# Dealing VectorE's work on a half out over the feed-forward slots, with clusters found a half ahead

## The chip, the cores and the metric

The kernel runs on one core of one Trainium2 chip. The metric is the device time of one execution in microseconds, the median of three runs. The engines are named as in the profile: PE is TensorE (PEld its weight loads), DVE is VectorE, ACT is ScalarE, POOL is GpSimd, SP issues the DMAs.

## The reference

Clustered attention is followed by a two-layer feed-forward network. Batch 4, 8 heads, 768 positions, head width 64, 16 clusters per head; feed-forward 3072 tokens, width 512, hidden width 2048.

```python
q_assign = argmax(einsum(q_n, c_n)); k_assign = argmax(einsum(k_n, c_n))   # nearest of 16 centroids
mask   = q_assign[:, :, :, None] == k_assign[:, :, None, :]
scores = where(mask, q @ k.T / sqrt(D), -1e9)
attn   = softmax(scores);  attn_out = attn @ v              # (B, H, S, D)
x = attn_out.transpose(0, 2, 1, 3).reshape(B * S, H * D)    # 3072 x 512
h = x @ w_in
g = maximum(h, 0) + alpha * minimum(h, 0)
out = g @ w_out
```

A query attends only to keys of its own cluster.

## The kernel before

**Tiling.** Two heads form a *pair* n; there are 16 pairs, four for each batch b. A pair's 768 queries are taken in two *halves* of 384. Scores are held transposed, keys on partitions: a *chunk* c (0 to 5) is 128 keys by 2 heads by 384 queries. For one half of one pair the work is:

- TensorE computes the six chunks of scores (L461), ScalarE takes their exponential into a tile E (L479, L482).
- VectorE masks E (L494): where the query's cluster differs from the key's, E becomes zero. Two instructions for each chunk, one for each head.
- TensorE weighs v with the masked E (`weigh`, L567).
- VectorE adds the six chunks up (`add_up`, L505 and L510, five adds), turns the sum in 32 by 32 blocks (L515) and reduces it along its rows (L518, `part`, called the row sums below).
- TensorE's small matmul `total` (L527) finishes the denominators from `part`; VectorE's `invert` (L537 to L544) takes reciprocals and turns them; `normalise` (L588) multiplies the weighed sum by them into xT.

In the first batch's pairs (n < 4) the mask is done by extra matmuls (L471) in place of L494.

**Feed-forward.** When the four pairs of one batch have done one half, 384 rows of xT are ready, and a queue `ffn` gets 28 *pieces* for them: 16 of `hidden(f)` (four matmuls L611; ScalarE makes gT and neg, L618 and L619; VectorE joins them by the slope, L603) and 12 of `final` (four matmuls L631; after two of them ScalarE copies the result to y, L637, or VectorE adds it to y, L639). The order is eight hiddens, six finals, eight hiddens, six finals. The slope of hidden f is issued in the piece of the next hidden, ahead of that one's ScalarE work, and in its own piece where f is the last of four. These pieces run during the attention of the next four halves, so that TensorE always has matmuls.

**Order.** The order of instructions on each engine is written out by hand (`manual_schedule`): each engine executes in the order of the code. Steps u count thirds of a half. There are two loops. The first (u up to 23) does the first batch, with the conversion of the double-precision weights spread over it. The second (u from 24, `TOGETHER`) does the other 24 halves, here called *visits*: three steps of five slots, of which a clump of attention work takes the first three. The clump holds the first three chunks' scores, the weighing of the visit before, the masks of those three chunks, the normalise of the visit before, and the adds; then the other three chunks' scores, masks, adds, turn and row sums. Twelve slots are left, numbered 1 to 12 here (two in step 0, five in step 1, five in step 2), and each may get a feed-forward piece. At 28 pieces over 48 slots, the usual places are slots 1, 2, 4, 6, 7, 9 and 11. `total` stands at the head of slot 8, `invert` at the end of slot 9. So visits alternate: seven hiddens, then one hidden with six finals.

**Preparation.** From the second batch on, each pair is prepared while earlier visits run, by pieces at fixed slots counted from its first step: its loads, then `prep_blocks` (VectorE turns q and k, two of L330, slots 10 and 11), `prep_sims` (TensorE, L348, slot 1, and one slot later VectorE's argmax over clusters, L356 to L370), `prep_clusters` (TensorE spreads the winning cluster over partitions, L393; ScalarE copies it, L397; VectorE makes the keys, L404 and L408), and `prep_queries` for each half (VectorE, L425, slots 10 and 11 of the visit before it, called the query turns). In the kernel before, sims stand in slot 1 and clusters in slot 5 of the visit just before the pair's first. `total`, `prep_sims` and `prep_clusters` share one PSUM bank (`ps_m`, one buffer); hiddens and finals rotate through two (`ps_f`), which also take the third and fourth chunk's scores.

Of the kernel before, what the change touches and what calls it, by code (L numbers as in the profile page):

```python
# [9 lines left out]
FP32 = mybir.dt.float32  # L10
# [4 lines left out]
ALU = mybir.AluOpType  # L15
AX = mybir.AxisListType
PS = bass.MemoryType.PSUM
P = 128
# [3 lines left out]
def kernel(  # L22
# [11 lines left out]
    nc = tc.nc  # L34
# [4 lines left out]
    NJ = S // P  # L39
    NCH = DM // P  # L40
    NF = DF // P
    HJ = NJ // 2
    HS = HJ * P
    SCALE = float(D) ** -0.5
    GROUP = 2
# [19 lines left out]
    accp = fast.enter_context(tc.tile_pool(name="accp", bufs=2))  # L65
    rdp = fast.enter_context(tc.tile_pool(name="rdp", bufs=1))
# [36 lines left out]
    Q = 32  # L103
# [41 lines left out]
    for g in range(P // Q):  # L145
        r = slice(g * Q, (g + 1) * Q)
        nc.gpsimd.tensor_copy(
            out=fold[r, :].rearrange("p (a i) -> p a i", i=Q),
# [178 lines left out]
    def prep_blocks(n, w):  # L327
        if w == 0:
            qkTs[n] = qkp.tile([P, NB * P], FP32, name="qkT")
        nc.vector.transpose(out=qkTs[n][:, w * S:(w + 1) * S],  # L330
                            in_=raw_qk[n, w].rearrange("p j h d -> p (j h d)"))
        square(n, w)
# [11 lines left out]
    def prep_sims(n):  # L344
        hp = pairs[n][1]
        ps = misc()
        for g in range(NG):
            nc.tensor.matmul(out=ps[g * W:(g + 1) * W, 0:HS],  # L348
                             lhsT=cT[:, hp * W:(hp + 1) * W],
                             rhs=qkTs[n][:, g * HS:(g + 1) * HS],  # L350
                             start=True, stop=True)
        later(1, lambda: prep_argmax(n, ps))
# [34 lines left out]
    def prep_clusters(n):  # L387


        first = firsts.pop(n)  # L390
        ps = misc()
        for g in range(NG):
            nc.tensor.matmul(out=ps[:, g * 2 * NX:(g + 1) * 2 * NX], lhsT=spread[:, g, :],  # L393
                             rhs=first, start=True, stop=True)
        every = fsp.tile([P, NG, GT, NG, 2], BF16, name="every")
        everys[n] = every
        later(1, lambda: nc.scalar.copy(every.rearrange("p g i r h -> p (g i r h)"),  # L397
                                        ps[:, 0:NG * 2 * NX]))
        later(2, lambda: prep_keys(n))
# [42 lines left out]
    def more_room():  # L442
        for raw in raw_tiles:
            e_tiles.insert(0, raw.rearrange("p n w -> p (n w)").bitcast(FP32)[
                :, 0:2 * HS].rearrange("p (h q) -> p h q", h=2))
# [39 lines left out]
    def last(m):  # L485

        return waiting[len(waiting) - m:]

    def mask(m):
        for n, half, c, E in last(m):  # L490
            if n < NCH:
                continue
            for h in range(2):
                nc.vector.scalar_tensor_tensor(  # L494
                    out=E[:, h, :], in0=aqs[n, half][:, h, :],
                    scalar=keys[n][:, NJ + c, h:h + 1],
                    in1=E[:, h, :], op0=ALU.is_equal, op1=ALU.mult)

    def add_up(m):

        n, half, c, _ = last(m)[0]
        E = [e for _, _, _, e in last(m)]
        if c == 0:
            acc = accp.tile([P, 2, HS], FP32, name="acc")
            nc.vector.tensor_tensor(out=acc, in0=E[0], in1=E[1], op=ALU.add)  # L505
            accs[n, half] = acc
            E = E[2:]
        acc = accs[n, half]
        for e in E:
            nc.vector.tensor_tensor(out=acc, in0=acc, in1=e, op=ALU.add)  # L510
        if c + m == NJ:


            accT = accp.tile([P, 2 * NX, Q], FP32, name="acc")
            nc.vector.transpose(out=accT.rearrange("p x i -> p (x i)"),  # L515
                                in_=acc.rearrange("p h q -> p (h q)"))
            part = rdp.tile([P, 2 * NX], FP32, name="part")
            nc.vector.tensor_reduce(out=part, in_=accT, axis=AX.X, op=ALU.add)  # L518
            parts[n, half] = part

    parts, totals = {}, {}

    def total(n, half):

        if (n, half) in parts:
            ps = misc()
            nc.tensor.matmul(out=ps[:, 0:2 * NX], lhsT=fold, rhs=parts.pop((n, half)),  # L527
                             start=True, stop=True)
            totals[n, half] = ps
# [134 lines left out]
    AHEAD = 4  # L664
# [3 lines left out]
    for (n, half), u in start_of.items():  # L668
        def at(step, slot, piece):
            prep_at.setdefault((step, slot), []).append(piece)  # L670
        if half == 0:
            load_at.setdefault(max(u - AHEAD - 3, -AHEAD), []).append(n)
            if n < NCH:
                for g in range(len(groups)):
                    at(u - 4, FIRST + g, lambda n=n, g=g: prep_features(n, g))
            else:
                for w in range(2):
                    at(u - 4, FIRST + w, lambda n=n, w=w: prep_blocks(n, w))
            at(u - 3, FIRST, lambda n=n: prep_sims(n))
            if n >= NCH:  # L680
                at(u - 2, FIRST, lambda n=n: prep_clusters(n))
        for h in range(2):
            at(u - 1, FIRST + h, lambda n=n, half=half, h=h: prep_queries(n, half, h))

# [15 lines left out]
    for u in range(-AHEAD, TOGETHER):  # L700
        for n in load_at.get(u, []):
            if n > 1:
                load(n)
        n, half, s = steps[max(u, 0)]
        prior = steps[max(u - 1, 0)]
        ended = u > 0 and prior[2] == SB - 1
        tick()
        if u >= 0:
            score(n, half, range(s * GROUP, (s + 1) * GROUP))
        tick()  # L710
        if ended:
            invert(*prior[:2])
        if u > 0:
            weigh(GROUP, denominators=u <= UB)
        if u >= 0:
            mask(GROUP)
        if ended:
            normalise(*prior[:2])
        if u >= UB:
            add_up(GROUP)  # L720
        if u == UB:
            early.clear()
            feed_block(u)
            whole = len(ffn) - KEEP
        take = (max(len(ffn) - KEEP - whole * (UB - 1 - u % UB) // UB, 0) if ffn else 0)
        converting = 0 if u < 0 else 1 + (u % 4 == 3) if u < UB else 1 + u % 2
        for i in range(SLOTS - FIRST):
            tick()
            feed(take * (i + 1) // 3 - take * i // 3)
            if (u, i) == (1 - AHEAD, 0):  # L730
                cT, alpha_neg = prepare_constants()
            prepare(u, FIRST + i)
            if i < converting:
                convert_next()
        if s == SB - 1 and u >= UB:
            total(n, half)
    assert not sources and not under_way and not unfinished[0]
    more_room()
    for u in range(TOGETHER, NS + 1):
        for n in load_at.get(u, []):  # L740
            load(n)
        if u < NS:
            n, half, s = steps[u]
        if s == 0 or u == NS:
            prior = steps[u - 1][:2]
            assert not unfinished[0]
            tick()
            if u < NS:
                score(n, half, range(0, NJ // 2), alone=NJ // 2 - 1)
            tick()  # L750
            invert(*prior)
            weigh(GROUP if u == TOGETHER else NJ)
            if u < NS:
                mask(NJ // 2)
            normalise(*prior)
            if u % UB == 0:
                feed_block(u)
                whole = len(ffn) - (NS - u <= UB)
            if u == NS:
                break  # L760
            add_up(NJ // 2)
            tick()
            score(n, half, range(NJ // 2, NJ), alone=NJ // 2)
            mask(NJ // 2)
            add_up(NJ // 2)
            slots = range(3, SLOTS)
        else:
            slots = range(SLOTS)
        for i in slots:
            tick()  # L770
            if s == 0:
                prepare(u, FIRST + i - 3)
            if (s, i) == (SB - 1, 0):
                total(n, half)
            at_slot = (u % UB) // SB * FREE + (s * SLOTS + i - 3)
            left = UB // SB * FREE - 1 - at_slot
            pieces = len(ffn) - (NS - u <= UB) - whole * left // (UB // SB * FREE)
            feed(max(pieces, 0))
            if (s, i) == (SB - 1, SLOTS - 1) and unfinished[0]:
                feed(1)  # L780
            if s > 0:
                prepare(u, i)
            if (s, i) == (SB - 1, 1):
                invert(n, half)
    assert not prep_at
    while due:
        tick()
    good = const.tile([P, 2], FP32, name="good")
# [169 lines left out]
```

## Time and profile before

| | |
|---|---|
| time, median of 3 runs | 1061.76 us (1061.55 to 1062.21) |
| span of the profiled execution | 1057.3 us |
| granted TensorE clock | 0.995 |
| first loop | 0 to about 209.7 us |
| second loop, 24 visits | 209.7 to about 967 us |
| last feed-forward block alone | from about 967 us |
| VectorE busy within 470 to 860 us | 267.0 of 390 us |
| TensorE busy within 470 to 860 us | 373.3 of 390 us |

How to read it: a profile line of the timeline gives start, length, engine, line, operation, tiles written and read, shapes and count; in square brackets stands the idle time of the engine before it and what ended that. In the list of waits a line tells who waited for whom: total, number of times, longest. A matmul in 32-bit floats appears as two records; their ends are modelled, and the next record normally starts before the last one's modelled end.

Durations on VectorE that the change touches, mean of one: mask 611 ns (L494), add 957 ns (L510), turn 978 ns (L515), row sums 952 ns (L518), slope 666 ns (L603), block turn 939 ns (L330), query turn 568 ns (L425), y sum 684 ns (L639).

### The profile page before, as it was taken

The page shows a single profiled execution, that of the slowest core. Times are in us where ns is not written, and L with a number is a line of the kernel's source. Part 1 is how long each engine was busy: PE and PEld are TensorE (multiplying, and loading weights), DVE is VectorE, ACT ScalarE, POOL GpSimd, SP SyncE. Part 2 cuts the span into 40 slices and gives each one's busy share as a digit, 9 for nine tenths or more (in the row PEclk, how much of TensorE's full clock was granted, in tenths as well). Part 3 has the DMA queues.
Part 4 walks back from the last instruction along what each step waited for, and adds up shares of the span by engine and source line. Part 5 has one row for each costly group of instructions (what it writes and reads, how often), then busy time and mean ns, then how long its engine had stood idle before and what let it go on. Part 6 is the DMA issues. An engine that isn't in the chain of part 4 may idle for free.

```text
span 1057.3 us, 10220 instructions
## 1 busy us (share of the span) xinstructions
PE 1008.8 (95%) x3827; PEld 488.5 (46%) x3827; DVE 679.3 (64%) x1155; ACT 346.4 (33%) x676; POOL 55.9 (5%) x71
## 2 busy tenths in 40 slices
PE   8999999789999999999999999999999999999997
PEld 4444444344444545444444454544444454544553
DVE  4896878778475756757777573767857576661111
ACT  5655434334331323323133241413333032330220
POOL 1332312200000000000000000000000000000000
PEclk9999999899999999999999999999999999999999
DMA  9542654020000230050000230014000000000000
GB/s 219 175 126 80 140 111 90 20 59 11 1 1 20 40 45 16 1 105 15 1 1 0 61 40 5 15 35 85 1 0 1 23 8 0 1 1 30 1 1 33
DMA packets 120936, 42.72 MB, mean 40 GB/s; under 512 B 113696, under 2 KB 113712, under 8 KB 120880
## 3 DMA queue, kind: packets, MB, share of 16 engines
q1 hardware_dynamic: 120704, 41.95, 18.5%
q8 instruction: 32, 0.52, 0.2%
q14 instruction: 24, 0.20, 0.1%
q10 hardware_dynamic: 176, 0.04, 0.0%
HBM read 35.69 MB, written 6.29 MB: 40 GB/s over the span
## 4 chain that ended last, share of the span: by engine, by line
PE 71%; DVE 24%; issue 1%; ACT 1%; DMA 1%; SPq 0%; POOL 0%; DVEq 0%; POOLq 0%; ACTq 0%
PE fps L631 24%; PE fps L611 24%; PE vps L567 11%; PE sps L461 7%; DVE acc L510 7%; DVE raw L494 3%; DVE E L494 2%; PE fps L461 2%; DVE acc L515 2%; DVE part L518 2%; DVE acc L505 1%; DVE gT L603 1%; PE sps L471 1%; PE fps L562 1%; DVE xT L588 1%
## 5 line engine op out<-in xcount | busy, mean ns | idle before, releaser
L631 PE MATMUL fps<-w_out_sb,gT 128*128 128x512 f32 x768 | 342.4, 598 | 14.8 <-DVE gT L603 8.2
L611 PE MATMUL fps<-xT,w_in_sb 128*128 128x384 f32 x1024 | 343.6, 491 | 2.8 <-DVE y L639 2.8
L611 PEld LDWEIGHTS fps<-xT,w_in_sb 128*128 128x128 f32 x1024 | 190.4, 190 | 144.1 <-ACT raw L482 4.4
L631 PEld LDWEIGHTS fps<-w_out_sb,gT 128*128 128x128 f32 x768 | 143.1, 190 | 192.6 <-issue 154.5
L618 ACT ACTIVATE gT<-fps 128x384 f32<-128x384 f32 x128 | 62.9, 491 | 270.3 <-PE fps L611 270.3
L603 DVE SCALAR_TENSOR_TENSOR gT<-neg,alpha_neg,gT 128x384 f32<-128x384 f32 x128 | 83.1, 666 | 97.9 <-ACT neg L619 97.5
L494 DVE SCALAR_TENSOR_TENSOR raw<-aq,key,raw 128x384 f32<-128x384 bf16 x160 | 87.3, 611 | 44.3 <-ACT raw L482 44.3
L461 PE MATMUL sps<-qkT 64*128 64x384 f32 x576 | 110.5, 502 | 0.0
L482 ACT ACTIVATE E<-sps 128x768 f32<-128x768 f32 x88 | 67.2, 813 | 82.2 <-PE sps L471 44.9
L494 DVE SCALAR_TENSOR_TENSOR E<-aq,key,E 128x384 f32<-128x384 bf16 x128 | 70.3, 611 | 20.5 <-ACT E L482 20.5
L567 PE MATMUL vps<-E,vt 128*64 128x384 f32 x448 | 81.4, 491 | 0.0
L639 DVE TENSOR_TENSOR y<-y,fps 128x512 f32<-128x512 f32 x30 | 20.5, 684 | 91.9 <-PE fps L631 91.9
L461 PEld LDWEIGHTS sps<-qkT 64*128 64x128 f32 x576 | 52.0, 187 | 51.3 <-issue 21.1
L510 DVE TENSOR_TENSOR acc<-acc,E 128x768 f32<-128x768 f32 x64 | 61.2, 957 | 19.1 <-ACT E L482 16.9
L619 ACT ACTIVATE neg<-fps 128x384 f32<-128x384 f32 x128 | 62.1, 485 | 16.6 <-DVE gT L603 16.6
L482 ACT ACTIVATE raw<-sps 128x768 f32<-128x768 f32 x56 | 42.9, 814 | 70.1 <-PE sps L461 70.1
L637 ACT COPY y<-fps 128x512 f32<-128x512 f32 x24 | 14.1, 586 | 141.7 <-PE fps L631 141.7
L567 PE MATMUL vps<-raw,vt 128*64 128x384 f32 x320 | 56.5, 491 | 0.0
L567 PEld LDWEIGHTS vps<-E,vt 128*64 128x64 f32 x448 | 30.4, 137 | 41.3 <-issue 41.1
L510 DVE TENSOR_TENSOR acc<-acc,raw 128x768 f32<-128x768 f32 x48 | 45.8, 955 | 1.1
L461 PE MATMUL fps<-qkT 64*128 64x384 f32 x192 | 41.4, 508 | 0.0
L588 DVE TENSOR_TENSOR xT<-vps,rd 128x384 f32<-128x384 f32 x32 | 17.8, 557 | 33.9 <-PE vps L567 33.4
(100 smaller groups left out, 663.7 us busy)
## 6 DMA issues: line engine op xcount, KB each, us to landing
raw<-in_moe_w_in_dram SPq DMA_DIRECT2D x16, 512.0 KB, 4.2
raw<-in_moe_w_out_dram SPq DMA_DIRECT2D x16, 512.0 KB, 3.6
vt<-in_v_dram SPq DMA_DIRECT2D x16, 384.0 KB, 4.8
out_dram<-y SPq DMA_DIRECT2D x24, 256.0 KB, 2.0
qk<-in_q_dram SPq DMA_DIRECT2D x48, 96.0 KB, 3.5
qk<-in_k_dram SPq DMA_DIRECT2D x48, 96.0 KB, 3.7
qk<-in_q_dram SPq DMA_DIRECT2D x8, 192.0 KB, 4.9
qk<-in_k_dram SPq DMA_DIRECT2D x8, 192.0 KB, 4.5
```

The costliest lines, as they stand in the source:

```text
L461: nc.tensor.matmul(out=bank(ps, h), lhsT=qkT[r:r + D, S + c * P:S + (c + 1) * P], rhs=qkT[r:r + D, half * HS:(half + 1) * HS], start=True, ...
L482: nc.scalar.activation(out=E, in_=ps[:, :, 0:HS], func=AF.Exp, scale=SCALE)
L494: nc.vector.scalar_tensor_tensor(out=E[:, h, :], in0=aqs[n, half][:, h, :], scalar=keys[n][:, NJ + c, h:h + 1], in1=E[:, h, :], op0=ALU.is ...
L510: nc.vector.tensor_tensor(out=acc, in0=acc, in1=e, op=ALU.add)
L515: nc.vector.transpose(out=accT.rearrange("p x i -> p (x i)"), in_=acc.rearrange("p h q -> p (h q)"))
L567: nc.tensor.matmul(out=po[r:r + D, 0:HS], lhsT=vts[n][:, h, c, :], rhs=e[:, h, :], start=(c == 0), stop=(c == NJ - 1))
L588: nc.vector.tensor_tensor(out=xTs[b, half][:, hp, :], in0=pos.pop((n, half))[:, 0:HS], in1=rds.pop((n, half)), op=ALU.mult)
L603: nc.vector.scalar_tensor_tensor(out=gs[f], in0=neg, scalar=alpha_neg[:, f:f + 1], in1=gs[f], op0=ALU.mult, op1=ALU.add)
L611: nc.tensor.matmul(out=ps[:, 0:HS], lhsT=w_in_sb[:, c, f * P:(f + 1) * P], rhs=xT[:, c, :], start=(c == 0), stop=(c == NCH - 1))
L618: nc.scalar.activation(out=gs[f], in_=ps[:, 0:HS], func=AF.Relu)
L619: nc.scalar.activation(out=neg, in_=ps[:, 0:HS], func=AF.Relu, scale=-1.0)
L631: nc.tensor.matmul(out=ps[:, 0:DM], lhsT=gs[f][:, i * P:(i + 1) * P], rhs=w_out_sb[:, f, :], start=on and f == f0, stop=off and f == f0 + ...
```

## The change

Its first part takes work of VectorE out of the clump of the second loop. The clump keeps the masks of the first three chunks and the normalise. The masks of the other three chunks, all five adds, the turn and the row sums go into a list `todo`, along with `total` and `invert`: twelve items, of which each of the visit's twelve slots does one at its end. So slots 1 to 3 mask chunks 3 to 5, slots 4 to 8 add, slot 9 turns, slot 10 takes the row sums, slot 11 has `total` and slot 12 `invert`. It is meant to let the feed-forward's slopes and y sums, and the argmax, through on VectorE without a long clump of attention work in front of them.

Its second part finds a pair's clusters earlier. Loads move from 7 to 9 steps ahead of the pair's first step, blocks from 4 to 7, sims from 3 to 6, clusters from 2 to 4. Sims are still in slot 1, now two visits ahead, and clusters in slot 10 of that same visit. Queries stay one step ahead. For the pairs next in line this moves some preparation into the first loop.

In the first loop only the form of the helpers changes (an add for each chunk; turn and row sums as functions of their own at the same place).

```diff
-            load_at.setdefault(max(u - AHEAD - 3, -AHEAD), []).append(n)
+            load_at.setdefault(max(u - (7 if n < NCH else 9), -AHEAD), []).append(n)
...
-                    at(u - 4, FIRST + w, lambda n=n, w=w: prep_blocks(n, w))
-            at(u - 3, FIRST, lambda n=n: prep_sims(n))
+                    at(u - 7, FIRST + w, lambda n=n, w=w: prep_blocks(n, w))
+            at(u - (3 if n < NCH else 6), FIRST, lambda n=n: prep_sims(n))
             if n >= NCH:
-                at(u - 2, FIRST, lambda n=n: prep_clusters(n))
+                at(u - 4, FIRST, lambda n=n: prep_clusters(n))
...
             if u < NS:
-                mask(NJ // 2)
+                for chunk in last(NJ // 2):
+                    mask(chunk)
             normalise(*prior)
...
-            add_up(NJ // 2)
             tick()
             score(n, half, range(NJ // 2, NJ), alone=NJ // 2)
-            mask(NJ // 2)
-            add_up(NJ // 2)
+            E = last(NJ)
+            for c in range(NJ // 2, NJ):
+                todo.append(lambda c=c, E=E: mask(E[c]))
+            for c in range(1, NJ):
+                todo.append(lambda c=c, E=E: add_up(E[c], E[c - 1]))
+            todo.append(lambda n=n, half=half: turn(n, half))
+            todo.append(lambda n=n, half=half: rows_sums(n, half))
+            todo.append(lambda n=n, half=half: total(n, half))
+            todo.append(lambda n=n, half=half: invert(n, half))
...
-            if (s, i) == (SB - 1, 0):
-                total(n, half)
...
-            if (s, i) == (SB - 1, 1):
-                invert(n, half)
-    assert not prep_at
+            todo.popleft()()
+    assert not prep_at and not todo
```

More of the change, by code (lines that the diff above doesn't have):

```diff
@@ L487, in last, with mask @@
         return waiting[len(waiting) - m:]
[L489 to L502, printed above, removed]
+    def mask(chunk):
+        n, half, c, E = chunk
+        if n < NCH:
+            return
+        for h in range(2):
+            nc.vector.scalar_tensor_tensor(
+                out=E[:, h, :], in0=aqs[n, half][:, h, :],
+                scalar=keys[n][:, NJ + c, h:h + 1],
+                in1=E[:, h, :], op0=ALU.is_equal, op1=ALU.mult)
@@ L503, in add_up @@
+    def add_up(chunk, former):
+        n, half, c, E = chunk
         if c == 0:
[L504 to L507, printed above, removed]
+            return
+        if c == 1:
+            accs[n, half] = accp.tile([P, 2, HS], FP32, name="acc")
         acc = accs[n, half]
-        for e in E:
-            nc.vector.tensor_tensor(out=acc, in0=acc, in1=e, op=ALU.add)
@@ L511, in add_up @@
[L511 to L519, printed above, removed]
+        nc.vector.tensor_tensor(out=acc, in0=former[3] if c == 1 else acc, in1=E,
+                                op=ALU.add)
@@ L521, with turn, rows_sums @@
+    def turn(n, half):
+        accT = accp.tile([P, 2 * NX, Q], FP32, name="acc")
+        nc.vector.transpose(out=accT.rearrange("p x i -> p (x i)"),
+                            in_=accs.pop((n, half)).rearrange("p h q -> p (h q)"))
+        accTs[n, half] = accT
+    def rows_sums(n, half):
+        part = rdp.tile([P, 2 * NX], FP32, name="part")
+        nc.vector.tensor_reduce(out=part, in_=accTs.pop((n, half)), axis=AX.X, op=ALU.add)
+        parts[n, half] = part
+    accTs = {}
     parts, totals = {}, {}
@@ L715 @@
         if u >= 0:
-            mask(GROUP)
+            for chunk in last(GROUP):
+                mask(chunk)
         if ended:
@@ L719 @@
         if u >= UB:
-            add_up(GROUP)
+            add_up(last(1)[0], last(2)[0]) if s == 0 else [
+                add_up(chunk, None) for chunk in last(GROUP)]
+            if s == SB - 1:
+                turn(n, half)
+                rows_sums(n, half)
         if u == UB:
@@ L738 @@
     more_room()
+    todo = deque()
     for u in range(TOGETHER, NS + 1):
@@ L753 @@
             if u < NS:
-                mask(NJ // 2)
+                for chunk in last(NJ // 2):
+                    mask(chunk)
             normalise(*prior)
```

## The prediction

> **What bounds the kernel now.** I read the page first, then the list of waits kept to TensorE, then the timeline round the places where those waits fall.[...]
>
> ```profile
> span 1057.3 us, 10220 instructions
> PE 1008.8 (95%) x3827; PEld 488.5 (46%) x3827; DVE 679.3 (64%) x1155; ACT 346.4 (33%) x676; POOL 55.9 (5%) x71
> ...
> q1 hardware_dynamic: 120704, 41.95, 18.5%
> ```
>
> TensorE sets the end: no other engine is over 64%, and the queue for loads is at 18.5%. The change takes no matmul away, so it can only win time in which TensorE stands still. The list of waits, TensorE alone, gives that time by cause (us in total, times, longest):
>
> ```profile
> PE mps L393 <- DVE first L370: 18.5, 10, 2.3
> PE fps L631 <- DVE gT L603: 8.2, 12, 1.0
> PE fps L631 <- POOL w_out_sb L253: 6.7, 2, 3.5
> PE fps L611 <- DVE y L639: 2.8, 2, 2.4
> ```
>
> Three of the four end on VectorE, an engine that is only 64% busy: VectorE is late in places, not short of time. Two stretches of the timeline (start, length, engine, line, operation) show why. The first is a visit with a new pair's clusters in it:
>
> ```profile
> 477.46 2.93 DVE L510 TENSOR_TENSOR acc<-acc,E 128x768 f32<-128x768 f32 x3
> ...
> 480.42 0.98 DVE L515 STREAM_TRANSPOSE acc<-acc 128x768 f32<-128x768 f32 x1
> ...
> 481.44 0.95 DVE L518 TENSOR_REDUCE part<-acc 128x24 f32<-128x768 f32 x1
> 482.31 0.57 DVE L356 STREAM_TRANSPOSE simT<-mps 128x384 f32<-128x384 f32 x1
> ...
> 484.49 0.55 DVE L370 TENSOR_REDUCE first<-top 128x24 bf16<-128x384 bf16 x1
> ...
> 485.10 0.26 PE L393 MATMUL mps<-first,spread 128*128 128x24 bf16 x4 [2.34 <-DVE first L370]
> ```
>
> The argmax (L356 to L370) stands behind the whole clump of sums, turn and row sums, and the cluster matmul of slot 5 stands waiting for it. The second is a visit of finals:
>
> ```profile
> 635.62 0.98 DVE L515 STREAM_TRANSPOSE acc<-acc 128x768 f32<-128x768 f32 x1
> ...
> 636.63 0.95 DVE L518 TENSOR_REDUCE part<-acc 128x24 f32<-128x768 f32 x1
> 637.50 1.14 DVE L603 SCALAR_TENSOR_TENSOR gT<-neg,alpha_neg,gT 128x384 f32<-128x384 f32 x2
> ...
> 638.16 8.85 PE L631 MATMUL fps<-w_out_sb,gT 128*128 128x512 f32 x20 [1.01 <-DVE gT L603]
> ```
>
> Here the two slopes, whose inputs ACT had finished at about 632.9, come behind turn and row sums, and the second final waits.
>
> [...] The operations keep their shapes, so I use the trace's durations.
>
> **What is removed.** The idle times count from a matmul's modelled end, though the next one normally starts before it: in a running stream records are 0.32 us apart and 0.49 us long. So each wait costs about 0.16 us more than listed: 18.5 + 10 x 0.16 = 20.1 for L393; 8.2 + 12 x 0.16 = 10.1 for the slopes, of which 0.4 lies at 98 us in the first loop and stays; 2.8 + 2 x 0.16 = 3.1 for the y sums.
> - L393: blocks still come one step before sims, but clusters now follow sims by nine slots (1 to 10), not four (1 to 5). VectorE's argmax (2.6 us) has the length of six feed-forward pieces, over 15 us, and no clump of sums in front of it. I take all 20.1 as gone.
> - Slopes: with mask, sums and turn out of the clump, VectorE is free after the normalise (600.92 in the visit that starts its pieces at 602.38). A slope now stands ahead of its own slot's dealt item, and slope 7 ahead of all of them, so it ends 4.4 us (3.75 until neg is ready, 0.65) after its hidden starts; the final that needs it starts at 2.6 + 3.4 = 6.0. All 9.7 gone.
> - y sums at 223 to 229 us, behind the first masked clump: gone for the same reason, 3.1.
> Sum removed: 33 us.
>
> **What is added.** The dealt items are the same instructions, so VectorE's 679 us stays. Turn and row sums, though, move from just after the clump to slots 9 and 10, and the total (TensorE, L527) from slot 8 to slot 11, straight behind them. TensorE now waits in order for row sums; behind it stand the last pieces and the next scores. I walk the instruction order of the changed kernel, with t = 0 at the first hidden. Hiddens follow each other every 2.58 us (ACT's L618 starts at 605.27, 607.85, 610.43), and neg of hidden k is ready at 3.75 + 2.58k (606.13 - 602.38 for the first). Back to back and with their hand-overs an add takes 0.99, turn 1.01, row sums 0.97, slope 0.60, query turn 0.58, block turn 0.95 (spacing of starts around 606 to 612; L330 for the last).
> - Five visits of seven hiddens: the fourth hidden's slope ends at 3.75 + 7.74 + 0.65 = 12.15. Then three adds, a slope, turn, a query turn, row sums: 2.97 + 0.60 + 1.01 + 0.58 + 0.97 = 6.13, so 18.3. TensorE reaches the total at 7 x 2.58 + 0.1 = 18.15. Wait 0.2 each, 1.0.
> - Four such visits that also hold sims, clusters and a block turn: TensorE 18.15 + 0.8 + 0.2 = 19.15; VectorE 18.3 + 0.8 + 0.95 = 20.05. Wait 0.9 each, 3.6.
> - Two visits where the total comes after six hiddens (the third and the last but one of the loop): VectorE 12.15 + two adds 1.98 + turn 1.01 + slope 0.60 + query 0.58 + row sums 0.97 = 17.3; TensorE 15.6. Wait 1.7 each, 3.4.
> - The loop's first visit, where the cluster matmul and the total follow the fifth hidden: 12.15 + 1.01 + 0.58 + 0.95 + 0.97 = 15.65 against 13.1. Wait 2.55.
> - Twelve visits with finals, 3.44 us each (eight records 0.43 apart): TensorE reaches the total at 2.6 + 6 x 3.44 = 23.2, in two of them after five finals at 19.8. VectorE is held by the second y sum until 17.2 (fourth final's end 16.4 and 0.7); two adds, turn, query and row sums bring it to 21.7, in the two without the adds to 19.8. No wait.
> Together 10.5 us. The later invert (reciprocal, minimum, two turns, 1.6 us) ends about 1 us into the next scores' masks; the normalise then still ends by the time the weighing does (626.9 in the trace), so it is hidden by the weighing. Earlier blocks, sims and clusters put 5.2 us more on VectorE in the first loop; its gap of 2.6 us at 155.2 and the next ones take it up, save 0.5 us in the step with the weights' wait (POOL, 6.7), where the keys now stand ahead of the last conversion: +0.5. Loads move two steps earlier and have a whole visit to land against 3.5 us; nothing.
>
> The unknown cost is the wait at the total. Bounds: zero in all visits, or one more dealt item (1 us) of lag in each of the twelve hidden visits.
>
> **The rivals.**
> 1. No wait at the total, since VectorE runs a little ahead of my walk: 1061.8 - 33 + 0.5 = 1029.3. For it: the five plain visits miss by only 0.2. Against: the fourth hidden's slope pins the rest.
> 2. VectorE lags more, because each dealt item stands behind a slope that waits for ACT: one more us in twelve hidden visits, 1039.8 + 12 = 1051.8.
> 3. A wait takes the place of the ones removed: the first visit's 2.55 us at the total in all 24 visits, 61 us, against 33 + 0.5 gained and paid: 1061.8 - 33 + 0.5 + 61 = 1090, slower. For it: the total now has one slot, not eight slots, of room behind row sums. Against: the walk leaves 1.5 us of room in ten of the twelve visits with finals.
>
> **How the numbers follow.** Forecast 1061.8 - 33 + 10.5 + 0.5 = 1039.8, chance 0.60. Rival 1: 0.14. Rival 2: 0.19. Rival 3, with milder forms that still end slower: 0.05; in between and unchanged, 0.02. The range takes rivals 1 and 2 at their ends, 1029 to 1052. Faster 0.93, same 0.02, slower 0.05.
>
> **What would show it.** Right: the list of waits has no cluster matmul on first and no final on gT past the first loop, and a new entry of the total's matmul on part, about 10 us, with its longest near 2.4 early in the second loop. TensorE's busy time stays within a few us of 1009. Wrong: that entry over 30 us, or new waits of hiddens on xT, of scores, or of weighing on masks; a gain under 10 us without such an entry would mean that the removed waits were no cause.

## The result, and the profile after

The changed kernel takes 1035.96 us (median of four runs, 1032.79 to 1039.08) against 1061.99 us: ratio 0.9754, 95% interval 0.9724 to 0.9785. That is 26 us gained. The two profiled executions are 22.7 us apart (spans 1057.3 and 1034.6 us): the profiled execution of the kernel before took 1059.04 us, 3 us under the median, at a granted clock of 0.995.

From the page of the changed kernel, the span and the busy times:

```profile
span 1034.6 us, 10221 instructions
PE 1007.1 (97%) x3827; PEld 494.2 (48%) x3827; DVE 674.6 (65%) x1155; ACT 345.5 (33%) x676; POOL 55.7 (5%) x71
```

Every engine has as many instructions as before and, within 1.2%, the same busy time; the span alone is shorter. So what went is time in which TensorE stood still. The list of TensorE's waits in the changed kernel (who waited for whom: us in total, times, longest):

```profile
PE fps L634 <- POOL w_out_sb L253: 7.0, 2, 3.6
PE mps L530 <- DVE part L520: 5.2, 7, 2.1
PE fps L614 <- POOL w_in_sb L253: 3.1, 1, 3.1
...
PE fps L634 <- DVE gT L606: 0.2, 1, 0.2
```

(L634, L614 and L530 are the finals, the hiddens and `total`, which were L631, L611 and L527.) The cluster matmul is gone from the list, and so are the hiddens behind a y sum; of the finals behind a slope one of 0.2 us at 98 us is left. Two entries are new: `total` waits for the row sums in seven visits, and one hidden waits for w_in in the first loop, that is for GpSimd's last step (L253) of converting a block of that weight.

A visit of the changed kernel with a cluster matmul in it, in order of time:

```profile
488.17 0.61 DVE L606 SCALAR_TENSOR_TENSOR gT<-neg,alpha_neg,gT 128x384 f32<-128x384 f32 x1
488.70 0.97 DVE L514 STREAM_TRANSPOSE acc<-acc 128x768 f32<-128x768 f32 x1
488.83 0.25 PE L393 MATMUL mps<-first,spread 128*128 128x24 bf16 x4
488.94 2.83 PE L614 MATMUL fps<-xT,w_in_sb 128*128 128x384 f32 x8
...
490.05 0.94 DVE L330 STREAM_TRANSPOSE qkT<-qk 128x768 f32<-128x768 f32 x1
...
490.91 0.91 DVE L520 TENSOR_REDUCE part<-acc 128x24 f32<-128x768 f32 x1
...
491.97 0.37 PE L530 MATMUL mps<-part,fold 128*128 128x24 f32 x2 [0.20 <-DVE part L520]
```

The cluster matmul has no bracket: it waits for nothing. The turn now stands near the visit's end, the block turn between it and the row sums, and `total` comes 0.20 us too early. In the second loop's first visit the same order costs ten times that:

```profile
240.91 0.62 DVE L606 SCALAR_TENSOR_TENSOR gT<-neg,alpha_neg,gT 128x384 f32<-128x384 f32 x1 [1.37 <-ACT neg L622]
241.45 0.97 DVE L514 STREAM_TRANSPOSE acc<-acc 128x768 f32<-128x768 f32 x1
...
242.39 0.25 PE L393 MATMUL mps<-first,spread 128*128 128x24 bf16 x4
...
243.66 0.91 DVE L520 TENSOR_REDUCE part<-acc 128x24 f32<-128x768 f32 x1
...
244.72 0.37 PE L530 MATMUL mps<-part,fold 128*128 128x24 f32 x2 [2.08 <-DVE part L520]
```

Here `total` follows the cluster matmul directly, while VectorE has waited until 240.91 for the fourth hidden's neg and has turn, a query turn, a block turn and row sums still to do.

### The profile page after: what moved, and what is told of

It is laid out like the page before. It is cut to its first block, busy times and chain, and to the rows that moved or that the text cites. A ratio compares the mean times of both kernels' runs of the same rounds, so it can differ in the third digit from the quotient of the medians.

```text
span 1034.6 us, 10221 instructions
## 1 busy us (share of the span) xinstructions
PE 1007.1 (97%) x3827; PEld 494.2 (48%) x3827; DVE 674.6 (65%) x1155; ACT 345.5 (33%) x676; POOL 55.7 (5%) x71
## 4 chain that ended last, share of the span: by engine, by line
PE 86%; DVE 8%; ACT 2%; issue 1%; DMA 1%; POOL 1%; SPq 0%; DVEq 0%; POOLq 0%; ACTq 0%
PE fps L634 31%; PE fps L614 28%; PE vps L570 11%; PE sps L461 9%; PE fps L461 4%; DVE acc L508 2%; PE fps L565 1%; PE sps L471 1%; PE mps L348 1%; DVE gT L606 1%; DVE acc L514 1%; DVE qkT L330 1%; DVE part L520 1%; DMA raw<-in_moe_w_in_dram 1%; PE mps L530 1%
## 5 line engine op out<-in xcount | busy, mean ns | idle before, releaser
L614 PE MATMUL fps<-xT,w_in_sb 128*128 128x384 f32 x1024 | 342.7, 492 | 3.1 <-POOL w_in_sb L253 3.1
L634 PE MATMUL fps<-w_out_sb,gT 128*128 128x512 f32 x768 | 337.1, 595 | 7.2 <-POOL w_out_sb L253 7.0
L614 PEld LDWEIGHTS fps<-xT,w_in_sb 128*128 128x128 f32 x1024 | 192.0, 191 | 147.6 <-issue 7.1
L634 PEld LDWEIGHTS fps<-w_out_sb,gT 128*128 128x128 f32 x768 | 144.8, 190 | 184.8 <-issue 166.1
L606 DVE SCALAR_TENSOR_TENSOR gT<-neg,alpha_neg,gT 128x384 f32<-128x384 f32 x128 | 86.2, 676 | 156.2 <-ACT neg L622 155.5
L570 PE MATMUL vps<-E,vt 128*64 128x384 f32 x448 | 81.5, 491 | 0.0
L570 PE MATMUL vps<-raw,vt 128*64 128x384 f32 x320 | 56.5, 491 | 0.0
L570 PEld LDWEIGHTS vps<-E,vt 128*64 128x64 f32 x448 | 30.5, 137 | 41.8 <-issue 41.0
L479 ACT ACTIVATE raw<-fps 128x384 f32<-128x384 f32 x48 | 21.0, 493 | 48.5 <-PE fps L461 48.5
```

Of the source, the lines that this page charges most:

```text
L479: nc.scalar.activation(out=E[:, h, :], in_=ps[h][:, 0:HS], func=AF.Exp, scale=SCALE)
L570: nc.tensor.matmul(out=po[r:r + D, 0:HS], lhsT=vts[n][:, h, c, :], rhs=e[:, h, :], start=(c == 0), stop=(c == NJ - 1))
L606: nc.vector.scalar_tensor_tensor(out=gs[f], in0=neg, scalar=alpha_neg[:, f:f + 1], in1=gs[f], op0=ALU.mult, op1=ALU.add)
L614: nc.tensor.matmul(out=ps[:, 0:HS], lhsT=w_in_sb[:, c, f * P:(f + 1) * P], rhs=xT[:, c, :], start=(c == 0), stop=(c == NCH - 1))
L634: nc.tensor.matmul(out=ps[:, 0:DM], lhsT=gs[f][:, i * P:(i + 1) * P], rhs=w_out_sb[:, f, :], start=on and f == f0, stop=off and f == f0 + ...
```

## The experiments

The theory: TensorE's waits came from the order of VectorE's queue, a clump that stood in front of short operations which TensorE needs. The main rival: the cluster waits, two thirds of the listed 29.5 us, went because clusters are found earlier. The first four runs split the change in two and take its two new costs away one at a time.

**The dealing alone.** The four distances of the preparation are put back:

```diff
-            load_at.setdefault(max(u - (7 if n < NCH else 9), -AHEAD), []).append(n)
+            load_at.setdefault(max(u - AHEAD - 3, -AHEAD), []).append(n)
...
-                    at(u - 7, FIRST + w, lambda n=n, w=w: prep_blocks(n, w))
-            at(u - (3 if n < NCH else 6), FIRST, lambda n=n: prep_sims(n))
+                    at(u - 4, FIRST + w, lambda n=n, w=w: prep_blocks(n, w))
+            at(u - 3, FIRST, lambda n=n: prep_sims(n))
...
-                at(u - 4, FIRST, lambda n=n: prep_clusters(n))
+                at(u - 2, FIRST, lambda n=n: prep_clusters(n))
```

> The dealing alone; loads, blocks, sims and clusters stay where the kernel before has them (clusters four slots after sims). Theory (the order on VectorE is the cause): with no clump of sums in front of it the argmax (2.6 us after slot 1's mask) is done long before slot 5, three pieces or over 7 us later, so L393 waits under 1 us in all; the waits of finals on gT and of hiddens on y go too; total waits on part 6 to 8 us; the w_in wait of 3.1 us in the first loop is gone, since the v loads are issued two steps later again. About 1034 us, like the changed kernel or 2 us better. Rival (finding the clusters earlier is what removes the cluster wait): L393 keeps some 18 us of waits, and the time is about 1054.

Measured: 1034.05 us (five runs, 1031.61 to 1035.13) against 1062.15, ratio 0.9732 (0.9710 to 0.9754). Its list of TensorE's waits begins:

```profile
PE mps L530 <- DVE part L520: 6.6, 7, 2.2
PE fps L634 <- POOL w_out_sb L253: 6.1, 2, 3.5
```

No cluster matmul waits, though clusters are as late as before, and the wait on w_in is gone. The theory holds and the rival falls: the dealing brings 28 us by itself, and no gain from adding the second part to it can be seen.

**The earlier preparation alone.** The kernel before with the second part of the change:

```diff
-            load_at.setdefault(max(u - AHEAD - 3, -AHEAD), []).append(n)
+            load_at.setdefault(max(u - (7 if n < NCH else 9), -AHEAD), []).append(n)
...
-                    at(u - 4, FIRST + w, lambda n=n, w=w: prep_blocks(n, w))
-            at(u - 3, FIRST, lambda n=n: prep_sims(n))
+                    at(u - 7, FIRST + w, lambda n=n, w=w: prep_blocks(n, w))
+            at(u - (3 if n < NCH else 6), FIRST, lambda n=n: prep_sims(n))
...
-                at(u - 2, FIRST, lambda n=n: prep_clusters(n))
+                at(u - 4, FIRST, lambda n=n: prep_clusters(n))
```

> The earlier loads, blocks, sims and clusters alone; masks, sums, turn and row sums stay in the clump, total in slot 8. Both theories: L393's 18.5 us of listed waits go. Theory: the finals' waits on gT (8.2 listed) and of hiddens on y (2.8) stay, and the w_in wait of about 3 us in the first loop appears as in the changed kernel: 1062 - 20 + 4 = about 1046 us. Rival (the waits are all of one kind and the earlier argmax frees VectorE for the slopes as well): gT waits under 3 us, about 1036.

Measured: 1050.04 us (1048.46 to 1051.37), ratio 0.9884 (0.9862 to 0.9906): 12 us gained, 4 fewer than the theory gave, and 14 short of what its rival gave. Its list of TensorE's waits:

```profile
PE fps L631 <- DVE gT L603: 9.0, 13, 1.0
PE fps L631 <- POOL w_out_sb L253: 7.0, 2, 3.5
PE fps L611 <- POOL w_in_sb L253: 3.4, 1, 3.4
PE fps L611 <- ACT neg L619: 3.2, 4, 0.8
PE fps L611 <- DVE y L639: 1.8, 2, 1.4
```

The cluster waits are gone and the slopes' stay, as expected. The fourth line was not expected, and the timeline shows where it comes from:

```profile
424.91 0.55 DVE L370 TENSOR_REDUCE first<-top 128x24 bf16<-128x384 bf16 x1
425.38 2.55 DVE L603 SCALAR_TENSOR_TENSOR gT<-neg,alpha_neg,gT 128x384 f32<-128x384 f32 x4
426.02 0.49 ACT L619 ACTIVATE neg<-fps 128x384 f32<-128x384 f32 x1 [2.32 <-DVE gT L603]
...
426.57 2.85 PE L611 MATMUL fps<-xT,w_in_sb 128*128 128x384 f32 x8 [0.81 <-ACT neg L619]
```

The slopes are held up behind the clump and the argmax; so ScalarE's neg, which has two buffers, waits 2.32 us for a slope, and a hidden waits for the PSUM bank that this neg has to empty. In the kernel before neg waited 2.32 us too in such a visit (until 485.60 us), but TensorE was then standing at the cluster matmul anyway (until 485.10). Taking one wait away laid the next one open. Its 3.2 us, with 0.16 us of overlap for each of the four, are about the 4 us that the theory's gain was too high by.

**The v load back at 7 steps.** The changed kernel, with the v load as a function of its own:

```diff
+        if n < NCH:
+            load_v(n)
+    def load_v(n):
...
+            if n >= NCH:
+                load_v_at.setdefault(max(u - 7, -AHEAD), []).append(n)
...
```

> The changed kernel with only the v load put back to 7 steps ahead, a line of its own; the q and k loads stay 9 steps ahead. Theory (the v load waits in SyncE's queue for the weighing that frees its buffer, and the weights' loads stand behind it): SyncE's stop of some 18 us before 176 us goes, the wait of a hidden on w_in (3.1 us) is gone, the wait on w_out stays near 7: 1036 - 3.3 = about 1032.5 us. Rival (the w_in wait comes from VectorE's extra block turns and argmax in the first loop): the wait stays within 1 us of 3.1 and the time within 1 us of the changed kernel.

In the changed kernel SyncE's queue near the wait on w_in reads, with its entry in SyncE's list of waits on top (the v load waited for a weighing 12 times):

```profile
SPq L125 <- PE vps L570: 202.8, 12, 27.1
...
155.74 2.47 SPq L119 DMA_DIRECT2D qk<-in_k_dram  x4
176.18 0.39 SPq L125 DMA_DIRECT2D vt<-in_v_dram  x1
176.67 2.08 SPq L230 DMA_DIRECT2D raw<-in_moe_w_out_dram  x4
```

and VectorE's and TensorE's:

```profile
182.23 0.43 DVE L235 TENSOR_SCALAR power<-raw 128x512 uint32<-128x512 uint32 x1 [3.86 <-DMA raw<-in_moe_w_out_dram]
...
180.39 2.10 PE L614 MATMUL fps<-xT,w_in_sb 128*128 128x384 f32 x6
185.59 0.59 PE L614 MATMUL fps<-xT,w_in_sb 128*128 128x384 f32 x1 [3.10 <-POOL w_in_sb L253]
```

SyncE issued nothing between 158.2 us (the pair's last k load) and 176.18, where the weighing (L570) of an older pair let its v buffer go; four loads of weights then came at once. VectorE stood 3.86 us for the first of them (until 182.23), and behind that in its queue was its part of the w_in conversion (L250, at 183.51), which GpSimd's part follows at 184.27 and the hidden at 185.59. With the v load later, SyncE's queue reads:

```profile
153.21 2.42 SPq L119 DMA_DIRECT2D qk<-in_k_dram  x4
155.72 16.25 SPq L235 DMA_DIRECT2D raw<-in_moe_w_out_dram  x3
176.08 0.38 SPq L130 DMA_DIRECT2D vt<-in_v_dram  x1
```

Three of those loads now go out before the v load. The wait on w_in is gone, the waits on w_out total 6.1 us and those of `total` still 5.2. Measured: 1030.48 us (1030.15 to 1034.61), ratio 0.9714 (0.9691 to 0.9738). The rival falls, since VectorE's extra work in the first loop is still there and the wait is not. The waits show this; the time is 5.5 us under the changed kernel's, but the two intervals overlap.

**Two items in the slots without a piece.** The changed kernel, with the row sums two slots earlier:

```diff
-            todo.popleft()()
+            slot = s * SLOTS + i - 2
+            for _ in range({3: 2, 5: 2, 9: 0, 10: 0}.get(slot, 1)):
+                todo.popleft()()
```

> The changed kernel with two dealt items in slots 3 and 5 and none in 9 and 10, so that the row sums come in slot 8; total and invert stay in 11 and 12. Theory (total waits only because the row sums are issued one slot ahead of it): the waits of total on part, 5.2 us listed over 7 visits, fall under 0.6, no new wait of finals on gT over 1 us: 1036 - 6 = about 1030 us. Rival (VectorE has no time left in those visits, wherever the items stand): total still waits 3 us or more, or the waits move to gT, and the time is within 2 us of the changed kernel.

Measured: 1029.09 us (1028.06 to 1030.45), ratio 0.9694 (0.9673 to 0.9714). The entry of `total` waiting on part is gone from TensorE's list, and nothing new waits on gT; the first visit alone keeps a wait, of another kind:

```profile
PE fps L634 <- POOL w_out_sb L253: 6.9, 2, 3.5
PE fps L614 <- POOL w_in_sb L253: 2.4, 1, 2.4
...
PE mps L530 <- ACT every L397: 1.0, 1, 1.0
```

There `total` follows the cluster matmul directly and has to wait until ScalarE has emptied their common bank. VectorE had the time; the row sums stood too late in its queue. The rival, by which 3 us or more of these waits stay, falls.

**Both mends, with either preparation.** The same two items on the dealing alone, and on the changed kernel with the later v load.

> The dealing alone (preparation where the kernel before has it) with two items in slots 3 and 5 and none in 9 and 10. Theory (both remaining costs of the changed kernel are separate: the row sums one slot ahead of total, and the v load in SyncE's queue): total's waits on part (6.6 us listed in the dealing alone) under 0.8, no wait on w_in, w_out near 6.5: 1034 - 7.7 = about 1026.5 us, faster than every kernel so far. Rival (with clusters four slots after sims, the denser slots 3 and 5 put the argmax late again): L393 waits 3 us or more, and the time is 1030 or above.

> The changed kernel with both mends: two items in slots 3 and 5, and the v load 7 steps ahead. Theory: the two gains add, 1036 - 5.5 - 7 = about 1024 to 1026 us; left are the waits on w_out near 6.5 and about 1 us at the first total of the second loop. Rival (they overlap): about 1029 us, as with the two items alone.

Measured: 1024.13 us (1024.06 to 1024.37), ratio 0.9646 (0.9627 to 0.9665), on the dealing alone; 1024.99 us (1024.49 to 1025.16), ratio 0.9653 (0.9634 to 0.9673), on the changed kernel. The two gains add. Of the first, the list of TensorE's waits begins:

```profile
PE fps L634 <- POOL w_out_sb L253: 6.3, 2, 3.5
PE fps L311 <- ACT qkT L315: 1.4, 3, 0.9
```

The 3 us of cluster waits that its rival expected are not in the list, and neither is a wait of `total` on part or of a hidden on y; of the finals behind a slope one of 0.2 us is left. Its median is the lowest of the study: the change's second part taken back, and the row sums earlier.

**Turn and row sums alone.** The kernel before, with only these two out of the clump:

```diff
...
+            if (s, i) == (1, 1):
+                turn(n, half)
+            if (s, i) == (1, 3):
+                rows_sums(n, half)
             if (s, i) == (SB - 1, 1):
                 invert(n, half)
```

> The kernel before with only turn (0.98 us) and row sums (0.95 us) taken out of the clump, into slots 4 and 6; masks, adds, total, invert and the whole preparation stay. Theory (each wait is the excess of the clump over the room behind it, so 1.93 us less in the clump takes 1.93 us from every wait): L393 2.34 falls to about 0.4 where it was longest and to nothing elsewhere, gT waits of 1.0 vanish, the y wait of 2.4 falls to 0.5; about 3 us of the 29.5 listed are left: about 1032 us. Rival (the masks and adds are what makes VectorE late, and turn and row sums only move): half of the waits stay or a wait of total on part takes their place, 1045 us or more.

Measured: 1035.46 us (1033.72 to 1037.96), ratio 0.9756 (0.9733 to 0.9779), as much as the whole change and 3.5 us short of what the theory gave. Its list of TensorE's waits:

```profile
PE mps L534 <- DVE part L525: 2.5, 1, 2.5
...
PE mps L393 <- DVE first L370: 1.7, 5, 0.3
...
PE fps L618 <- DVE y L646: 0.9, 2, 0.5
```

The longest cluster wait fell from 2.3 to 0.3 and the longest y wait from 2.4 to 0.5, each by about the 1.93 us that left the clump, and past the first loop no final waits on gT. So the clump was too long by about the length of these two, and that accounts for most of the old waits. It does not make masks and adds in the clump free: this kernel is 11 us slower than the dealing with the row sums earlier. Its three lines above, which that kernel lacks, are 5.1 us of it; the slow matmuls after the longest wait (last section) belong to it too, and the rest was not located. The first line was not expected. In one late visit `total` follows the fourth hidden, and row sums in slot 6 stand behind that hidden's slope, which waits for ScalarE; it is the same fault as in the changed kernel: row sums that stand too late for `total`.

## Why the prediction was right, and where it was off

1039.8 us was forecast and 1035.96 measured: 22 us of gain against 26.

- *TensorE's standing time bounds the kernel, VectorE is late and not short of time*: right. VectorE's busy time went from 679.3 to 674.6 us, and the waits went. The two items moved inside the visit, at no less work for VectorE, show it again.
- *Removed, 33 us*: right in sum; the three entries left the list, but for the slope at 98 us that was forecast to stay. The prediction gave two reasons for the cluster waits, more slots and no clump in front. Each suffices alone: the dealing without more slots takes these waits away, and so does the earlier preparation with the clump in place. The change had both, so the two gains could not add.
- *Wait of `total` on part, 10.5 us*: the right wait in the right visits, and none in the visits with finals, as forecast; its size was too large. With the 0.16 us of overlap for each, the list gives 5.2 + 7 x 0.16 = 6.3. The first visit cost 2.08 + 0.16 = 2.24 (forecast 2.55), the two where it follows six hiddens 1.3 each (1.7), those with sims and block turn 0.20 + 0.16 = 0.36 (0.9), and the five plain visits nothing (0.2). The mis-sized term is the spacing on VectorE. The walk gave nearly every instruction its full length and a hand-over (turn 1.01, slope 0.60, query turn 0.58, block turn 0.95). In the changed kernel starts lie closer where an instruction does not need the one before it: 0.89 after the turn and 0.46 after the query turn (488.70, 489.59, 490.05), 0.86 after the block turn (490.91), 0.50 after a slope (308.06 to 308.56). The turn's 1.01 came from the kernel before, where the row sums, which need it, follow it directly (635.62 to 636.63). In the visit where `total` waits until 310.02, the row sums end 4.7 us after the fourth hidden's slope, and the walk had 5.14. (A slip of 0.1 without effect: for the visits with finals, 16.4 and 0.7 make 17.1, not 17.2.)
- *Loads: "nothing"*: wrong, by 3.1 + 0.16 us. The prediction asked whether the loads would land in time and not what stands behind them in SyncE's queue. The v load waits for TensorE (issued at 176.18 us, 18 us after the k load before it), and the loads of weights wait behind the v load (issued from 176.67 us on).
- *+0.5 us at the last conversion*: the wait on w_out went from 6.7 to 7.0.
- *Later `invert`, hidden by the weighing*: right; neither weighing nor hiddens wait for it in the list.

The wrong sizes partly cancel: 4.2 us less at `total`, 3.3 more at w_in. That the total came so close is to that extent luck. With the measured sizes the sum is 33 - 6.3 - 3.3 - 0.3, about 23 us, and the two profiled executions are 22.7 apart. The rest of the difference to the 26 us between the medians is about what the runs themselves vary by (6.3 us over four runs of the changed kernel, 6.1 over eleven of the one before), and that goes with the granted clock (last section).

## What to carry to other kernels

Where an engine takes its work in the order of the code, as VectorE did here (in the earlier preparation alone four slopes left from 425.38 us on, behind turn, row sums and argmax, and a neg waited 2.32 us for them), look at what stands between an operation that the bounding engine needs and the head of the queue, not at the share of busy time: 1.93 us out of a clump were worth as much here as dealing most of it out at first was (27 and 26 us). The dealing alone was worth 38 once the row sums stood three slots ahead of `total`. When work moves later, its consumer has to move by as much or the producer has to stand well before it; a row sum one slot ahead of its matmul became the largest wait that the change added (5.2 us). And the v load that waited for its buffer until 176.18 us held up the four loads of weights behind it in SyncE's queue: ask of each prefetch moved earlier what it may block.

## What the runs showed of the hardware that was not expected

After the 2.08 us wait in the second loop's first visit, the eight matmul records of the next hidden took 4.52 us where 2.83 is usual: six of them, from 245.70 us on, started 0.64 us apart where 0.32 is usual. The table by stretches of the changed kernel shows it in the granted clock (after the stretch come its length, then busy time and count for PE, PEld, DVE, ACT and POOL, PEclk, DMA share, GB/s):

```profile
244.93 4.52 PE L614 MATMUL fps<-xT,w_in_sb 128*128 128x384 f32 x8
...
221.00:243.00 22.00, 21.64 (x74) 11.15 (x70) 15.17 (x25) 5.74 (x14) 0.00 (x0) 1.00 0.19 42
243.00:250.00 7.00, 5.28 (x14) 2.89 (x16) 5.23 (x11) 1.10 (x5) 0.00 (x0) 0.76 0.00 0
```

So that wait cost some 1.7 us more than its own length. Over 236 to 252 us the mean clock was 0.89 in the changed kernel and in the dealing alone, whose list has a longest wait of `total` of 2.2 us, and 1.00 in the kernel before and with the two items. In the kernel with only turn and row sums out of the clump, the first two matmul records of the hidden after its 2.5 us wait, from 839.85 us on, took 1.63 us; those of the changed kernel's hidden at 488.94 us took 0.89. It isn't a rule in these runs: after the cluster wait of 2.34 us at 300.2 us in the kernel before, the clock stayed at 1.00 (296 to 306). Nor is it the length alone: the wait on w_in of 3.1 us left the changed kernel at 1.00 (182 to 190), and the 2.08 us were followed by 0.76. And at the waits on w_out where the second loop begins the clock stood at 0.50 for 5 us (205 to 210 us in the kernel before, 210 to 215 in the changed one); over 205 to 221 us its mean was 0.81 and 0.68 in these two, 0.75 in the dealing alone and 0.68 with the two items. What sets it was not tried; no list of waits contains it.

The times of one kernel go with this clock. Of the eleven runs of the kernel before that stand beside the first experiments, the four at a mean clock of 0.989 took 1064.07 to 1064.52 us, the four at 0.992 took 1060.90 to 1062.15, and the one at 0.995 took 1058.45. A clock 0.006 lower over some 1060 us is 6.4 us of work by estimate, about the whole spread of 6.1. The runs of the kernel with the fewest waits lie closest together (1024.06 to 1024.37 us over five), and so do their clocks, 0.993 to 0.994. Why the clock differs from one run of a kernel to the next was not tried.
